# First MLP's weights read once and kept as 32-bit floats; Fourier folds by rows of 96

## The chip, the cores and the metric

The kernel runs on one core of one Trainium2 chip. The metric is the device time of one launch in microseconds (us), the median of three runs. The engines are named as the profile names them: PE (TensorE, matmuls), DVE (VectorE), ACT (ScalarE), POOL (GpSimd) and SP (SyncE, which only issues transfers). Each engine works its own instructions strictly in order; an instruction that waits holds up all that stand behind it on that engine.

## What is computed

Four batches of 768 tokens, 8 heads of 48, so 384 channels. A delta rule along the sequence gives the attention's output; then come two blocks with an MLP of 384 to 1536 to 384 channels each. The first mixes tokens by a product of rank 32 ahead of its MLP, the second by the real part of a two-dimensional Fourier transform, and normalises.

```python
for t in range(S):                                  # attention, delta rule
    kt, vt, bt = k_n[:, :, t], v[:, :, t], beta[:, :, t, None]
    y[:, :, t] = einsum('bhd,bhde->bhe', q[:, :, t], state)
    v_old = einsum('bhde,bhd->bhe', state, kt)
    state = state + bt[:, :, :, None] * einsum('bhd,bhe->bhde', kt, vt - v_old)
...
u = x + (x.transpose(0, 2, 1) @ U @ V).transpose(0, 2, 1)      # first block
x = u + np.maximum(u @ w_ch1, 0.0) @ w_ch2
...
u = x + np.real(fft(fft(x, axis=1), axis=2))                   # second block
un = (u - mean(u)) / sqrt(var(u) + 1e-06)
out = u + np.maximum(un @ w_ch1, 0.0) @ w_ch2
```

The weights U, V, `w_ch1` and `w_ch2` are stored as 64-bit floats.

## The kernel before

**Order.** Streams (Python generators, one for each kind of work) yield the modelled cost of their next instruction, and a planner (`Weave`) picks at every step which stream goes on, by modelled engine times, a bias for each stream and prices. The result is a fixed row of instructions for each engine. Rings and tiles set further waits when the program runs.

**Attention.** It has 24 chunks of 128 tokens (4 batches of 6). For each, K and Q are loaded (`s_load`, L692), normalised and folded by POOL and ACT (`s_front`), turned by transposing transfers into `BT` and `KT` (`s_turn`, L741 and L743, issued by SP) and copied (`K`, L752). Products of keys follow on PE (`ps_g`, L791 and L792), triangular blocks are spread by masks on DVE (L839: `bd`, `nf`, `t`) and the chunk is solved (`s_solve`). Its last step writes `U`; the text counts the solves by that step.

**First MLP's weights.** The two matrices have 24 pieces of 128 x 384 64-bit floats, 384 KB each; with three pieces of U and V, loads 0 to 2, that makes 3 + 24 + 24 = 51 loads. `weight_streams` has one stream that fetches into a ring `wst` of three slots (L447, issued by SP, each when the slot of the third load before is free) and one that converts. The 24 pieces go through the ring twice. In the first pass DVE looks for the largest absolute value (`peak`, L382); `weight_peak` makes a power of two for each matrix out of these. In the second pass `from_f64` makes a 32-bit float out of the two words of each value by three operations on DVE (L291, L294, L297), into `wf` or, up to late in the attention, into a PSUM scratch tile `wfp`; then the ring slot is free. `split` makes the pair of 16-bit floats that the MLP multiplies with: the high half `wh` on ACT (L364), the remainder `wl` on DVE (L367), or on ACT and POOL (L369, L370).

**First MLP.** It works on 8 blocks of 384 tokens beside the attention. For each of 12 steps PE makes `ps_h` (L1146), ACT its positive part `hh` (L1152), DVE the remainder `hl` (L1159), and PE adds the products into `acc` (L1176). The ring `wst` shares the buffer of the second block's input, so that block waits for the weights' last conversions (`s_mix`, L1245).

**Second MLP's weights.** `weight2_streams` reads its 24 pieces once: converted into tiles that stay, squared and summed on ACT (L491, the sum is read by an instruction of its own), scaled by one norm for each matrix (`weight_scale`), split in a row.

**Fourier folds.** For each batch, `fold` forms sums and differences of rows that mirror each other, in two halves i = 0 and 1 of up to 97 rows. It loads forward rows by SP and mirrored rows by POOL's gathers (L1408, one row for each partition by a table of row numbers), adds and subtracts on POOL (`pm`, L248), and ACT (L1398) and DVE (L1400) make the pair `fs`, which PE multiplies with tables (L1432). The last part of the second block (`u`, L1562; output transfers, L1569) and `s_in` (gathers `x1f`, L1408) use POOL's queue too.

Of the kernel before, what the change touches and what calls it, by code (L numbers as in the profile page):

```python
# [9 lines left out]
F32 = mybir.dt.float32  # L10
# [30 lines left out]
NP = 27  # L41
# [18 lines left out]
CU, CW1 = 7, 2  # L60
# [150 lines left out]
class Builder:  # L211
# [39 lines left out]
    def setup(self):  # L251
# [28 lines left out]
        self.wpk, self.wpk2, self.wsc1, self.unscale1 = some(2, KF), some(2), some(2), some(1)  # L280
# [4 lines left out]
    def from_f64(self, raw, f, n=HALF, sb=False):  # L285
# [11 lines left out]
        nc.vector.scalar_tensor_tensor(out=f, in0=hi, scalar=0xC0000000, in1=f,  # L297
                                       op0=ALU.bitwise_and, op1=ALU.bitwise_or)
        return f.bitcast(F32)
# [73 lines left out]
    def weight_parts(self, w1, w2):  # L373

        src = [(q, nm, j, k, x) for j in range(4) for q, (nm, xs) in enumerate(self.weight_sources(w1, w2, j)) for k, x in enumerate(xs)]

        def part(x, conv):
            return [(lambda raw: raw, self.words(x), 1092)], conv
# [6 lines left out]
        def conv(raw, done, q, nm, j, k):  # L385
            if k == 0:
                self.pair(self.wts, f"{nm}h{j}", 0, nm, j)
            sb = self.late = self.late or ("sol", NC - 2) in self.wv.mark
            f = yield from self.from_f64(raw, self.f64_tile(), sb=sb)
            done()  # L390
# [4 lines left out]
        peaks = [part(x, lambda raw, done, q=q, j=j, k=k: peak(raw, done, q, 3 * j + k)) for q, _, j, k, x in src]  # L395
        return peaks, [part(x, lambda raw, done, q=q, nm=nm, j=j, k=k: conv(raw, done, q, nm, j, k)) for q, nm, j, k, x in src]

    def weight_peak(self):

        nc = self.nc  # L400
        pk, s = self.wpk2, self.wss1
        yield {"v": 90}
        nc.vector.tensor_reduce(out=pk, in_=self.wpk, op=ALU.max, axis=AX.X)
        t = yield from self.take()
        ps = self.psu.tile([128, 130], F32, tag="psu", name="ps_w")
        yield {"p": 112}
        nc.tensor.transpose(ps[0:2, 0:128], pk, self.id32)
        top = self.wtot1
        yield {"v": 200}
        nc.vector.tensor_reduce(out=top[0:2, 0:1], in_=ps[0:2, 0:128], op=ALU.max, axis=AX.X)  # L410
        hi, p = (top[0:2, i:i + 1] for i in range(2))
        yield {"v": 70}
        nc.vector.tensor_scalar(out=p.bitcast(U32), in0=hi.bitcast(U32), scalar1=3, scalar2=0x3FFFFFFF, op0=ALU.logical_shift_left, op1=ALU.bitwise_and)
        yield {"v": 70}
        nc.vector.scalar_tensor_tensor(out=p.bitcast(U32), in0=hi.bitcast(U32), scalar=0x40000000, in1=p.bitcast(U32), op0=ALU.bitwise_and, op1=ALU.bitwise_or)
        yield {"v": 70}
        nc.vector.tensor_scalar(out=p, in0=p, scalar1=2.0 ** -60, scalar2=None, op0=ALU.max)
        yield {"v": 70}
        nc.vector.tensor_scalar(out=p.bitcast(U32), in0=p.bitcast(U32), scalar1=0x7F800000, scalar2=None, op0=ALU.bitwise_and)
        yield {"v": 70}  # L420
# [15 lines left out]
    def weight_streams(self, parts, bias):  # L436
# [1249 lines left out]
```

## Time and profile before

| | |
|---|---|
| median of 3 runs | 1136.72 us (1131.61 to 1137.6) |
| profiled run, time | 1134.32 us |
| profiled run, span of the trace | 1132.2 us |
| mean granted TensorE clock | 0.94 |
| busy in the span | PE 83%, DVE 66%, ACT 48%, POOL 30% |

The durations in this document are those of the one profiled execution. Its time is 2.1 us more than its span, and 2.4 us under the median of the runs. In the rows, an arrow in brackets ([9.81 <-DMA K<-KT]) gives the engine's idle time just before an instruction and what ended it; where an instruction waits for several things, it is the one that came last.

### The profile page before, as it was taken

The page shows a single profiled execution, that of the slowest core. Times are in us where ns is not written, and L with a number is a line of the kernel's source. Part 1 is how long each engine was busy: PE and PEld are TensorE (multiplying, and loading weights), DVE is VectorE, ACT ScalarE, POOL GpSimd, SP SyncE. Part 2 cuts the span into 40 slices and gives each one's busy share as a digit, 9 for nine tenths or more (in the row PEclk, how much of TensorE's full clock was granted, in tenths as well). Part 3 has the DMA queues.
Part 4 walks back from the last instruction along what each step waited for, and adds up shares of the span by engine and source line. Part 5 has one row for each costly group of instructions (what it writes and reads, how often), then busy time and mean ns, then how long its engine had stood idle before and what let it go on. Part 6 is the DMA issues. An engine that isn't in the chain of part 4 may idle for free. (4 is left out here: it accounts for less than half of the span.)

```text
span 1132.2 us, 25277 instructions
## 1 busy us (share of the span) xinstructions
PE 940.7 (83%) x10128; PEld 629.2 (56%) x10128; DVE 750.3 (66%) x1746; ACT 547.7 (48%) x1335; POOL 336.6 (30%) x319
## 2 busy tenths in 40 slices
PE   0377777359999888998999596899988899999998
PEld 0145655237766566766777254456656466565664
DVE  6478877889899888899984367874324453544432
ACT  4378888447665666666462133467412121222221
POOL 3322222014343233443300460365362531102010
PEclk9998787569999999999999888999999899999999
DMA  9999796837547576376322445532101411211210
GB/s 232 267 235 166 162 195 116 199 70 144 119 97 125 113 159 128 76 157 119 63 55 55 139 136 137 145 86 36 46 25 36 72 41 39 60 36 51 62 35 22
DMA packets 232974, 120.48 MB, mean 106 GB/s; under 512 B 198540, under 2 KB 218328, under 8 KB 232856
## 3 DMA queue, kind: packets, MB, share of 16 engines
q1 hardware_dynamic: 226440, 111.56, 45.9%
q0 software_dynamic: 6416, 7.30, 2.3%
q8 instruction: 79, 1.29, 0.5%
q14 instruction: 39, 0.32, 0.1%
HBM read 63.89 MB, written 14.16 MB: 69 GB/s over the span
## 5 line engine op out<-in xcount | busy, mean ns | idle before, releaser
L1176 PE MATMUL acc<-w2s,hh 128*128 128x384 f16 x1152 | 285.7, 330 | 7.8 <-DVE u L1562 5.2
L1146 PEld LDWEIGHTS <-w1s 128*128 128x128 f16 x1728 | 164.5, 99 | 137.4 <-issue 42.8
L1159 DVE SCALAR_TENSOR_TENSOR hl<-ps_h,hh 128x384 f16<-128x384 f32 x192 | 106.2, 553 | 176.0 <-ACT hh L1152 175.7
L1152 ACT ACTIVATE hh<-ps_h 128x384 f16<-128x384 f32 x192 | 93.5, 488 | 240.8 <-PE ps_h L1146 237.4
L1146 PE MATMUL ps_h<-u,w1s 128*128 128x384 f16 x864 | 176.1, 336 | 32.3 <-DVE hl L1159 23.3
L1176 PE MATMUL acc<-w2s,hl 128*128 128x384 f16 x576 | 189.6, 329 | 3.6 <-DVE hl L1159 3.6
L1146 PE MATMUL ps_h<-uh,w1s 128*128 128x384 f16 x864 | 159.7, 329 | 0.0
L1176 PEld LDWEIGHTS <-hh 128*128 128x128 f16 x1152 | 107.5, 100 | 70.0 <-issue 6.1
L248 POOL TENSOR_TENSOR GPl<-g,GPh 128x512 f16<-128x512 f32 x63 | 76.1, 1208 | 174.2 <-ACT GPh L241 161.7
L859 PEld LDWEIGHTS <-bd 128*128 128x128 f16 x1728 | 72.0, 99 | 49.2 <-DVE bd L839 21.8
L1176 PEld LDWEIGHTS <-hl 128*128 128x128 f16 x576 | 56.8, 99 | 43.2 <-DVE hl L1159 4.8
L792 PE MATMUL ps_g<-K,BT 128*128 128x256 f16 x192 | 55.1, 307 | 15.5 <-DMA K<-KT 15.5
L791 PE MATMUL ps_g<-KT,BT 128*128 128x256 f16 x192 | 54.8, 304 | 10.3 <-DMA KT<-kq 7.0
L248 POOL TENSOR_TENSOR pair<-x1f,pair 128x384 f16<-128x384 f32 x24 | 22.5, 938 | 130.2 <-ACT pair L1532 130.2
L248 POOL TENSOR_TENSOR pm<-xq 97x768 f32<-97x768 f32 (+1 forms) x16 | 28.9, 1821 | 88.3 <-DMA xq<-x1d 59.3
L798 DVE TENSOR_TENSOR g<-ps_g,mask 128x512 f32<-128x512 f32 x64 | 43.7, 683 | 6.7 <-PE ps_g L792 5.5
L248 POOL TENSOR_TENSOR kq<-kq,kq 128x384 f16<-128x384 f32 x45 | 44.7, 1010 | 10.2 <-ACT kq L241 4.8
L248 POOL TENSOR_TENSOR kb<-kq,rb 128x384 f32<-128x384 f32 x20 | 17.0, 849 | 91.2 <-DVE rb L653 57.5
L859 PE MATMUL lanes<-R,bd 128*128 128x32 f16 x768 | 34.8, 179 | 6.5 <-ACT R L241 3.7
L839 DVE TENSOR_TENSOR bd<-Xc,mmask 128x1024 f16<-128x1024 f16 x48 | 36.9, 768 | 4.5 <-ACT Xc L893 4.2
L241 ACT ACTIVATE GPh<-g 128x512 f16<-128x512 f32 x61 | 37.9, 623 | 3.7 <-DVE g L798 3.3
L248 POOL TENSOR_TENSOR kb<-kb,kb 128x384 f16<-128x384 f32 x21 | 19.9, 949 | 66.2 <-ACT kb L241 65.2
(268 smaller groups left out, 1921.5 us busy)
## 6 DMA issues: line engine op xcount, KB each, us to landing
wst<-in_moe_w_ch_dram SPq DMA_DIRECT2D x72, 384.0 KB, 3.6
K<-KT SPq DMA_DIRECT2D x48, 256.0 KB, 4.5
kq<-in_k_dram SPq DMA_DIRECT2D x24, 192.0 KB, 3.9
kq<-in_q_dram SPq DMA_DIRECT2D x24, 192.0 KB, 4.2
vt<-in_v_dram SPq DMA_DIRECT2D x24, 192.0 KB, 3.9
xnd<-vt SPq DMA_DIRECT2D x24, 192.0 KB, 2.1
xn<-xnd SPq DMA_DIRECT2D x24, 192.0 KB, 2.9
x1d<-u SPq DMA_DIRECT2D x24, 192.0 KB, 1.9
```

The costliest lines, as they stand in the source:

```text
L241: self.nc.scalar.activation(out=out, in_=in_, func=ACTF.Copy)
L248: (self.nc.vector if eng == "v" else self.nc.gpsimd).tensor_tensor(out=out, in0=in0, in1=in1, op=op)
L791: nc.tensor.matmul(o, BT[:, h, :], KT[:, :, h, :], start=i == 0, stop=False, skip_group_check=True)
L792: nc.tensor.matmul(o, BT[:, h, :], K2[:, :, h, :], start=False, stop=True, skip_group_check=True)
L798: nc.vector.tensor_tensor(out=g32.rearrange("p i (a t) -> p (i a) t", a=2), in0=ps.rearrange("p i (a t) -> p (i a) t", a=2), in1=self.mask ...
L839: self.nc.vector.tensor_tensor(out=dst.rearrange("p h (j c) -> p h j c", j=n), in0=x, in1=mask[:, None, :, :].to_broadcast(shape), op=ALU. ...
L859: nc.tensor.matmul(ps[:, h, :], lhs[:, h, :], rhs[:, h, :], start=plus is None, stop=plus is None or h == H - 1)
L1146: nc.tensor.matmul(ps[:, i, :], w[:, k, fs], u[x][:, k, :], start=(m == 0), stop=(m == 3 * KD - 1))
L1152: nc.scalar.activation(out=hh, in_=ps, func=ACTF.Relu)
L1159: nc.vector.scalar_tensor_tensor(out=hl, in0=ps, scalar=0.0, in1=hh, op0=ALU.max, op1=ALU.subtract)
L1176: nc.tensor.matmul(acc, h[:, ds_], w, start=(f == 0 and j == 0), stop=(f == KF - 1 and j == 2))
```

## The change

**Weights.** Each piece is read once. `keep` converts it; the first two of the three operations go into the scratch tile as before, the third writes a stored tile `w{p}` of 32-bit floats for the pair p. ACT squares the float into the ring slot and sums it, and then the slot is free. After the 24th piece `weight_scale` makes one norm for each matrix, and `pairs` splits the 21 stored pieces in a row; the pair p is written in the tile of stored pair p - 1. The last pair (three pieces of `w2`) is read first, for its norm alone, and once more at the end (`again`), where its split follows at once. There are 30 loads instead of 51, and the second block waits for the last of them. `CU` and `CW1` are exponents of the scales, changed for the norm.

**Folds.** Both halves load and gather 96 rows (before, the first half had loads of 97 and 96 rows and gathers of 97, the second loads of 1, 95 and 95 rows and gathers of 96). Row 192 (S/4) goes to partition 96 of the first half, by a transfer of one partition that brings both of its forward values; the other two stay zero. The transfers and gathers of a fold remain five and four. The table of row numbers follows, and the planner is told 500 and 100 ns for the loads where it was told 820.

```diff
-CU, CW1 = 7, 2
+CU = 5
...
+        out = f if out is None else out
+        nc.vector.scalar_tensor_tensor(out=out, in0=hi, scalar=0xC0000000, in1=f,
...
-        def peak(raw, done, q, i):
-            yield {"v": _v(HALF)}
-            self.nc.vector.tensor_reduce(out=self.wpk[:, q, i:i + 1], in_=raw[:, :, 1].bitcast(F32), op=ALU.max, axis=AX.X, apply_absolute_value=True)
+        def keep(raw, done, p, k):
+            j, q = divmod(p, 2)
+            if p < last and k == 0:
+                stored[p] = self.wts.tile([128, 3, HALF], U32, tag=f"w{p}", name="wf3")
+            t = tile_of()
+            f = yield from self.from_f64(raw, t, sb=self.late, out=stored[p][:, k, :] if p < last else None)
+            yield {"a": _a(HALF) + 200}
+            nc.scalar.activation(out=raw.rearrange("p n t -> p (n t)")[:, 0:HALF].bitcast(F32), in_=f, func=ACTF.Square,
+                                 accum_out=self.wpk[:, q, 3 * j + k:3 * j + k + 1])
             done()
...
+                self.pair(self.wts, f"w{(p - 1) % len(src)}", 0, nm, j)
             yield from self.split(0, nm, j, k, f, self.wsc1[:, q:q + 1], sb)
...
+        def again(raw, done, p, k):
+            t = tile_of()
+            f = yield from self.from_f64(raw, t, sb=self.late)
+            done()
+            yield from split(p, k, f, self.late)
+
+        def pairs():
+            yield from self.weight_scale(None, self.wpk, self.wsc1, self.unscale1, CW, CW, (self.wtot1, self.wss1))
+            self.wv.post("wscale1")
+            for p in range(last):
+                for k in range(3):
+                    yield from split(p, k, stored[p][:, k, :].bitcast(F32), True)
...
+        return [part(x, keep, p, k) for p in [last, *range(last)] for k, x in enumerate(src[p][1])], [part(x, again, last, k) for k, x in enumerate(src[last][1])]
...
-                    yield from self.weight_peak()
+                    yield from self.pairs()
...
-                yield ("conv", 2 * NP - 4)
+                yield ("conv", self.loads - 1)
...
+                nc.gpsimd.memset(x[96:97], 0.0)
...
-        rows = [[(0, 97, 0, 0), (1, 97, 3, HALF + 1)], [(0, 1, 0, S // 4), (1, 96, 0, 97), (1, 96, 3, HALF + 97)]]
...
-            for lo, hi, y, at in rows[i]:
-                yield _d(820)
-                nc.sync.dma_start(x[lo:hi, y, :], x1[at:at + hi - lo])
+            for y in (0, 3):
+                at = 96 * i + HALF * (y // 3)
+                yield _d(500)
+                nc.sync.dma_start(x[0:96, y, :], x1[at:at + 96])
+            if i == 0:
+                yield _d(100)
+                nc.sync.dma_start(x[96:97, 0:3:2, :], x1[S // 4:3 * S // 4 + 1:HALF])
             for y in range(2):
-                yield from self.gather(b, x[0:k, 1 + y, :], KD * B + 2 * i + y)
+                yield from self.gather(b, x[0:96, 1 + y, :], KD * B + 2 * i + y)
```

**What it moves.** The lines of the changed kernel are numbered 8 to 12 lower from `weight_streams` on (L447 is L435, L839 is L827, L1408 is L1400). First, SP's row at the start, from the first transposing transfer to the first copy of K. Before:

```order
L741 DMA_TRANSPOSE BT<-kb_131 128x8x128
L447 DMA wst<-in_moe_w_ch_dram 128x768 x2
L743 DMA_TRANSPOSE KT<-kq_127 128x16x128
L447 DMA wst<-in_moe_w_ch_dram 128x768
L692 DMA kq<-in_k_dram 128x8x48
L692 DMA kq<-in_q_dram 128x8x48
L447 DMA wst<-in_moe_w_ch_dram 128x768 x2
L752 DMA K_308<-KT 64x2048 x2
```

After:

```order
L729 DMA_TRANSPOSE BT<-kb_131 128x8x128
L731 DMA_TRANSPOSE KT<-kq_127 128x16x128
L435 DMA wst<-in_moe_w_ch_dram 128x768
L680 DMA kq<-in_k_dram 128x8x48
L680 DMA kq<-in_q_dram 128x8x48
L740 DMA K_299<-KT 64x2048 x2
```

Before, three more weight loads stand before the first transposing transfer and five between it and the first copy of K, eight in all; after, three and one.

Second, DVE's row between the sixth and the seventh solve, where L367 (after: L368) is the second half of a split, L291 to L297 are a conversion and L839 (after: L827) spreads the attention's blocks by a mask. Before:

```order
L367 SCALAR_TENSOR_TENSOR w1s<-wf,few,w1s 128x384
L291 TENSOR_SCALAR wf<-wst 128x384
L294 SCALAR_TENSOR_TENSOR wf<-wst,wf 128x384
L297 SCALAR_TENSOR_TENSOR wf<-wst,wf 128x384
L839 TENSOR_TENSOR nf_144<-Nc,mmask 128x1024
L367 SCALAR_TENSOR_TENSOR w1s<-wf,few,w1s 128x384
L291 TENSOR_SCALAR wf<-wst 128x384
L294 SCALAR_TENSOR_TENSOR wf<-wst,wf 128x384
L297 SCALAR_TENSOR_TENSOR wf<-wst,wf 128x384
L839 TENSOR_TENSOR t_151<-Tc,mmask 128x512
L367 SCALAR_TENSOR_TENSOR w2s<-wf,few,w2s 128x384
```

After:

```order
L368 SCALAR_TENSOR_TENSOR w1s<-wf_1706,few,w1s 128x384
L827 TENSOR_TENSOR nf_144<-Nc,mmask 128x1024
L368 SCALAR_TENSOR_TENSOR w1s<-wf_1706,few,w1s 128x384
L827 TENSOR_TENSOR t_151<-Tc,mmask 128x512
L368 SCALAR_TENSOR_TENSOR w2s<-wf_2586,few,w2s 128x384
L243 COPY t_151<-Zs 32x8x32
L931 STREAM_TRANSPOSE nf_144<-Zs 32x8x32
L368 SCALAR_TENSOR_TENSOR w2s<-wf_2586,few,w2s 128x384
L931 STREAM_TRANSPOSE nf_144<-Zs 32x8x32
L368 SCALAR_TENSOR_TENSOR w2s<-wf_2586,few,w2s 128x384
L1148 SCALAR_TENSOR_TENSOR hl<-ps_h,hh 128x384
```

Before, splits and conversions alternate here; after, the conversions stand further ahead and only splits are left. Counted from the start to the sixth solve, DVE has before 24 searches for the largest value, 9 conversions and 8 splits of these weights, after 24 conversions and no split (10 of the 24 ahead of the first solve, where before stand the 24 searches alone). From there to the third `hl` it has before 15 conversions and 14 splits, after 3 and 23.

Third, POOL's row in the fold of the third batch, where `xq` are the gathers, the three rows of `pm` the sums, `out_dram` output transfers. Before:

```order
L1408 DMA xq_11544<-x1d_85,rows 97x384 x2
L248 TENSOR_TENSOR pm<-xq_11544 97x2x384 x2
L248 TENSOR_TENSOR pm<-pm 97x2x191 x2
L248 TENSOR_TENSOR pm<-pm 97x2x193 x2
L1408 DMA xq_11545<-x1d_85,rows 96x384 x2
L248 TENSOR_TENSOR pm<-xq_11545 96x2x384 x2
L248 TENSOR_TENSOR pm<-pm 96x2x191 x2
L248 TENSOR_TENSOR pm<-pm 96x2x193
L1569 DMA out_dram<-u_12282,rows 3072x384
L1569 DMA out_dram<-u_12434,rows 3072x384
L1569 DMA out_dram<-u_12587,rows 3072x384
```

After:

```order
L1400 DMA xq_11493<-x1d_85,rows 96x384 x2
L248 TENSOR_TENSOR pm<-xq_11493 97x2x384 x2
L248 TENSOR_TENSOR pm<-pm 97x2x191 x2
L248 TENSOR_TENSOR pm<-pm 97x2x193 x2
L1400 DMA xq_11494<-x1d_85,rows 96x384 x2
L248 TENSOR_TENSOR pm<-xq_11494 96x2x384 x2
L248 TENSOR_TENSOR pm<-pm 96x2x191 x2
L248 TENSOR_TENSOR pm<-pm 96x2x193 x2
L1561 DMA out_dram<-u_12287,rows 3072x384
L1561 DMA out_dram<-u_12440,rows 3072x384
L1561 DMA out_dram<-u_12560,rows 3072x384
```

The gathers have 96 rows each, and the last sum of the second half, which stood behind three output transfers and a gather of `x1f`, stands ahead of them.

## Rows read from the trace of the kernel before

**Rows 1.** Page: busy sums; the span in 40 slices of 28.3 us.

```profile
PE 940.7 (83%) x10128; PEld 629.2 (56%) x10128; DVE 750.3 (66%) x1746; ACT 547.7 (48%) x1335; POOL 336.6 (30%) x319
...
PE   0377777359999888998999596899988899999998
...
GB/s 232 267 235 166 162 195 116 199 70 144 119 97 125 113 159 128 76 157 119 63 55 55 139 136 137 145 86 36 46 25 36 72 41 39 60 36 51 62 35 22
```

**Rows 2.** Busy time by stage: start and end, length, engines, clock, DMA share, GB/s.

```profile
core 0: us, PE busy (x) PEld busy (x) DVE busy (x) ACT busy (x) POOL busy (x), PEclk, DMA share, GB/s
0.00:86.30 86.30, 32.05 (x311) 18.40 (x312) 54.12 (x135) 45.85 (x108) 27.99 (x38) 1.00 1.03 244
86.30:193.70 107.40, 82.23 (x1429) 63.86 (x1427) 86.60 (x212) 91.58 (x237) 25.72 (x30) 0.81 0.88 164
193.70:255.30 61.60, 29.28 (x312) 19.36 (x312) 52.61 (x110) 31.48 (x71) 8.21 (x8) 0.59 0.57 129
255.30:620.00 364.70, 338.88 (x5278) 243.82 (x5276) 314.40 (x717) 221.42 (x547) 116.55 (x107) 1.00 0.56 109
620.00:740.00 120.00, 87.34 (x510) 53.33 (x509) 76.72 (x157) 41.02 (x117) 40.84 (x30) 0.89 0.48 134
740.00:1132.00 392.00, 370.86 (x2297) 230.44 (x2295) 165.86 (x421) 116.36 (x258) 117.32 (x108) 0.98 0.19 46
```

**Rows 3.** Timeline at the start, SP's queue and PE: start, length, instruction, idle before.

```profile
29.14 2.17 SPq L447 DMA_DIRECT2D wst<-in_moe_w_ch_dram  x2
...
39.61 0.40 PE L792 MATMUL ps_g<-K,BT 128*128 128x256 f16 x1 [9.81 <-DMA K<-KT]
```

**Rows 4.** Costs by line (sum, ns each); last two: DVE reading `wst`, by stretch.

```profile
L382 DVE TENSOR_REDUCE few<-wst 128x1 f32<-128x384 f32 x24 | 12.8, 545 | 16.9 <-DMA wst<-in_moe_w_ch_dram 16.9
...
L367 DVE SCALAR_TENSOR_TENSOR w2s<-wf,few,w2s 128x384 f16<-128x384 f32 x8 | 5.2, 654 | 1.3 <-ACT w2s L364 1.2
...
L364 ACT ACTIVATE w1s<-wfp,few 128x384 f16<-128x384 f32 x5 | 2.9, 576 | 0.0
...
L491 ACT ACTIVATE wst<-wf 128x384 f32<-128x384 f32 x24 | 12.5, 520 | 21.6 <-DVE wf L297 21.6
...
L491 ACT ACTIVATION_READ_ACCUMULATOR wst<-wf 128x1 f32 x24 | 4.5, 189 | 0.0
...
86.30:193.70 107.40, 14.72 (x27) 0.00 (x0) 0.81 0.88 164
193.70:242.30 48.60, 22.21 (x45) 0.00 (x0) 0.54 0.61 149
```

**Rows 5.** Timeline of the first fold, POOL, ACT and PE.

```profile
628.26 2.47 POOL L1408 DMA_INDIRECT xq<-x1d,rows  x1 [0.30 <-issue]
642.84 3.70 POOL L248 TENSOR_TENSOR pm<-xq 97x768 f32<-97x768 f32 x2 [12.11 <-DMA wst<-in_moe_w_ch_dram]
646.49 4.61 POOL L248 TENSOR_TENSOR pm<-pm 97x382 f32<-97x382 f32 x4
...
652.48 1.44 POOL L1408 DMA_INDIRECT xq<-x1d,rows  x1 [0.30 <-issue]
...
651.13 0.94 ACT L1398 ACTIVATE fs<-pm,few 97x772 f16<-97x772 f32 x1 [13.99 <-POOL pm L248]
...
653.74 3.04 PE L1146 MATMUL ps_h<-u,w1s 128*128 128x384 f16 x9 [13.09 <-DVE hl L1159]
```

**Rows 6.** Transfers issued, us to landing: gathers of 97 rows (877 to 883), then 96 (898 to 902).

```profile
xq<-x1d,rows POOLq DMA_INDIRECT x2, 10.5
...
xq<-x1d,rows POOLq DMA_INDIRECT x2, 3.1
```

**Rows 7.** Timeline of PE beside the folds of the third and fourth batch.

```profile
829.52 0.50 PE L1176 MATMUL acc<-w2s,hh 128*128 128x384 f16 x2 [2.37 <-ACT hh L1152]
...
854.43 0.50 PE L1432 MATMUL ps_d<-ce,fs 96*128 96x193 f16 x2 [3.70 <-ACT fs L1398]
...
901.89 0.80 PE L1176 MATMUL acc<-w2s,hh 128*128 128x384 f16 x2 [5.16 <-DVE u L1562]
```

More of the change, by code (lines that the diff above doesn't have):

```diff
@@ L373, in weight_parts, with part, tile_of, split @@
     def weight_parts(self, w1, w2):
-        src = [(q, nm, j, k, x) for j in range(4) for q, (nm, xs) in enumerate(self.weight_sources(w1, w2, j)) for k, x in enumerate(xs)]
-        def part(x, conv):
-            return [(lambda raw: raw, self.words(x), 1092)], conv
-        def peak(raw, done, q, i):
-            yield {"v": _v(HALF)}
-            self.nc.vector.tensor_reduce(out=self.wpk[:, q, i:i + 1], in_=raw[:, :, 1].bitcast(F32), op=ALU.max, axis=AX.X, apply_absolute_value=True)
+        nc = self.nc
+        src = [p for j in range(4) for p in self.weight_sources(w1, w2, j)]
+        last = len(src) - 1
+        stored = {}
+        def part(x, conv, p, k):
+            return [(lambda raw: raw, self.words(x), 1092)], lambda raw, done: conv(raw, done, p, k)
+        def tile_of():
+            self.late = self.late or ("sol", NC - 2) in self.wv.mark
+            return self.f64_tile()
+        def keep(raw, done, p, k):
[7 more added lines that the diff above has]
+                                 accum_out=self.wpk[:, q, 3 * j + k:3 * j + k + 1])
             done()
-        def conv(raw, done, q, nm, j, k):
+        def split(p, k, f, sb):
+            j, q = divmod(p, 2)
+            nm = src[p][0]
             if k == 0:
[L387 to L390, printed above, removed]
+                self.pair(self.wts, f"w{(p - 1) % len(src)}", 0, nm, j)
             yield from self.split(0, nm, j, k, f, self.wsc1[:, q:q + 1], sb)
@@ L393, in conv @@
                 self.wv.post("weights", 0, nm, j)
[L395 to L420, printed above, removed]
-        nc.vector.tensor_scalar(out=s[0:2], in0=self.id32[0:2, 0:2], scalar1=p, scalar2=None, op0=ALU.mult)
-        yield {"p": 112}
-        nc.tensor.matmul(ps[:, 128:130], self.ones[0:2], s[0:2], start=True, stop=True)
-        yield {"a": 95}
-        nc.scalar.activation(out=s, in_=ps[:, 128:130], func=ACTF.Copy)
-        self.give(t)
-        yield {"v": 70}
-        nc.vector.tensor_scalar(out=self.unscale1, in0=s[:, 0:1], scalar1=s[:, 1:2], scalar2=2.0 ** -(CW1 + CW), op0=ALU.mult, op1=ALU.mult)
-        yield {"v": 70}
-        nc.vector.reciprocal(out=self.wsc1, in_=s)
-        for q, c in enumerate((CW1, CW)):
-            yield {"v": 70}
-            nc.vector.tensor_scalar(out=self.wsc1[:, q:q + 1], in0=self.wsc1[:, q:q + 1], scalar1=2.0 ** c, scalar2=None, op0=ALU.mult)
-        self.wv.post("wscale1")
@@ L502, in weight2_streams, with weight_scale @@
         return [Stream(x(), bias) for x in (fetch, convert)]
-    def weight_scale(self, pool, squares, scale, unscale, c1, c2):
+    def weight_scale(self, pool, squares, scale, unscale, c1, c2, few=None):
         nc = self.nc
-        tot, s = (pool.tile([128, 2], F32, name=x) for x in ("wtot", "wss"))
+        tot, s = few or (pool.tile([128, 2], F32, name=x) for x in ("wtot", "wss"))
         yield {"v": 75}
@@ L1115, in attention @@
         parts = self.mix_parts() + peaks + weights
+        self.loads = len(parts)
         self.wst = self.weight_streams(parts, (WB, WB))
```

17 lines of the change are left out of this document (8 added, 9 removed).

## The prediction

> **What bounds the kernel now.** I read the page first: TensorE (PE) is busy 83% of the span, and the slices show where the other 17% lies: in the first eleven slices and again around slices 22 to 26 [rows 1]. The table of stages makes that exact [rows 2]: from 255 to 620 us PE is busy 338.9 of 364.7 us and from 740 us on 370.9 of 392, so little is to be had there except at single holes. Up to 255 us it is busy only 143.6 us, and from 620 to 740 87.3 of 120. In the first stage the transfers are the limit (DMA share 1.03, 244 GB/s). In the second VectorE (DVE) is busy 86.6 and ScalarE (ACT) 91.6 of 107.4 us: the attention's small operations and the weights share them. In the third DVE is busy 52.6 of 61.6 us and PE 29.3, at a granted clock of 0.59. So the weights matter in the first 255 us, and the Fourier folds in the holes after 620 us. The changed kernel's order tells which operations move, the trace what they cost.
>
> **Part A, the start (0 to 86 us).** The ring takes three loads at a time, and SP issues in order. Before, eight weight loads stand ahead of the first K copy; after, four (order of SP). The last two of them are issued from 29.14 us on, right ahead of K, and PE waits 9.81 us for K [rows 3]. Four loads of 393,216 bytes at the 267 GB/s of the second slice [rows 1] are 5.9 us. Against this, the 24 searches for the largest value (545 ns each, 12.8 us of DVE) go, and ten conversions with ten squares come ahead of the same point: 10 x 1.64 = 16.4 us of DVE (a conversion is three operations, 14.72 us / 9) and 10 x (0.520 + 0.189) = 7.1 of ACT [rows 4]. That is +3.6 us on a DVE that is busy 54 of 86 us, and the searches also waited 16.9 us for their loads [rows 4], so I let the slack take it. Bounds 0 (the transposes' own time sets the start) and -8 (most of the 9.81 us); I take **-5**, near the bytes.
>
> **Part B, 86 to 194 us** (up to the sixth of the 24 chunks' solves). Before, 9 conversions and 8 splits of weights stand here; after, 14 conversions with squares and no split. DVE: 14 x 1.64 less (14.7 + 8 x 0.65 for the second half of a split), that is 23.0 - 19.9 = +3.1 us. ACT: 14 x 0.709 less 8 x 0.58 (the first half), 9.9 - 4.6 = +5.3 us [rows 4]. Five more loads move 2.0 MB where the DMA share is 0.88 [rows 2]. ACT is the fuller engine, 85% busy, and I put its whole excess on the path: **+5**; bounds 0 (slack takes it) and +12 (both engines' excess, and 0.7 us of wait for each of the five loads, the 16.9 / 24 of the searches).
>
> **Part C, 194 to 255 us** (to the third `hl`, the first output block of the MLP). Before, 15 conversions (22.2 us) and 14 splits on DVE (14 x 0.65 = 9.1), 31.3 us in all; after, 3 conversions (3 x 1.48 = 4.4, from the 22.2 us of 45 operations) and 23 splits (15.0), 19.4 us [rows 4]. DVE is the busiest engine of this stage, and PE waits on the attention's chains behind it, so the 11.9 us go nearly whole. ACT gets 9 more first halves, 5.2 us, and stays below DVE: 31.5 + 5.2 of 61.6 [rows 2]. The new wait is that the 21 stored pieces can't be split until the norm is known, and that each pair is written over the stored piece ahead of it: the ACT half of a pair stands behind the DVE half of the pair before. Behind a split that waits so, DVE's order has the attention's masks and transposes, and the next chunk waits for these; 7 borders of about 1.2 us (0.58 + 0.65) would give back 8 us. Bounds -16 (the chain of the stage also tightens) and -4; I take **-11**. The last pair is read a second time at the end, 3 loads of 393 KB, counted in the 3 conversions. From there to 620 us both kernels' rows run alike and PE is full: nothing.
>
> **Part E, the first fold (625 to 654 us).** GpSimd (POOL) issues a gather of 97 rows in 2.47 us at 628.26 and then waits 12.11 us until its first sum at 642.84. The two sums take 8.3 us, ACT's `fs` starts at 651.13 having waited 13.99 us, and the MLP's `hh`, which is queued behind that `fs` on ACT, comes late, so PE stands 13.09 us [rows 5]. The view names `wst` as POOL's last releaser, but the load alone is not the gather. Gathers of 97 rows land 10.5 us after issue, those of 96 rows 3.1 [rows 6], and the small gather is issued in 1.44 us [rows 5]. With both gathers at 96 rows the landing comes 7.4 us sooner and the two issues 2 us sooner, so **-9** of the 13.09. Bounds -12 (all but about 1 us of the hole) and -3 (the two loads of 384 KB and the tables queued at the same time hold the gather up, whatever its rows).
>
> The Trainium skill, page DMA: Bandwidth & Descriptors, section "Why a DMA increments its semaphore by 16 and not by 1", says that a transfer is spread over the largest number of engines up to 16 that divides its outer dimension: 96 partitions on 16 engines, a prime such as 97 on one. The landings above agree with that. The same section names an exception, by which some of GpSimd's direct copies use 16 engines whatever the count; by it the gathers would gain nothing, and parts E to G would be about 0.
>
> **Parts F and G, the later folds.** The folds of batches 2 and 3 stand beside the second MLP, and PE waits there 2.37 us at 829.52 and 5.16 at 901.89 (`fs` of the first half late, `hh` behind it) [rows 7]. A landing 7.4 us sooner covers both: **-7.5** (bounds -7.5 and 0). In the second half PE waits 3.70 us at 854.43 for `fs` [rows 7]. Before, the last sum on POOL stands behind three output transfers and an `x1f` gather; after, in front of them (order of POOL): **-4**. Bounds -4 and +4, since those output transfers go out later, and `u` buffers come free later by about the same.
>
> The zero rows, the extra row of 96 and the shorter planner costs don't cost anything that I can find: five transfers and four gathers per fold stay, the one-row transfer replaces one of the same kind, and the memset of a single partition stands at the start of the folds.
>
> **Sum.** -5 + 5 - 11 - 9 - 7.5 - 4 = -31.5 us. Against the profiled run, 1134.3 us (1132.2 of span and 2.1 around it), that is 1102.8. The median of the three runs lies 2.4 us higher, at 1136.7: **1105** on that scale. All lower ends together give -47.5 (1089), all upper ends +9 (1146); both are unlikely together, and the range is set below.
>
> **Rivals.** About 0.5% (5.7 us) is what a measurement can tell from no change: faster is below 1131.0, slower above 1142.4.
> - *The first fold's hole stays* because the loads and tables queued with it, not the 97 rows, set its landing. For: POOL's wait is put down to `wst` [rows 5]. Against: the same gather takes 10.5 us in a stretch with hardly another transfer [rows 6]. Without E: 1105 + 9 = 1114. Chance 0.12.
> - *The weights bring nothing*: what C gives back is lost in A and B, with DVE and ACT as busy there as [rows 2] shows. For: ACT's 85%. Against: the count of operations to 255 us falls on DVE by 5 us (+3.6 + 3.1 - 11.9). The folds' -20.5 remains: 1116. Chance 0.12.
> - *The folds bring nothing*: the holes come from the sums' 8.3 us, which stay, or a gather's landing doesn't depend on its count of rows and the 10.5 us were the other transfers'. For: the sums are the longest single step of [rows 5]. Against: 10.5 and 3.1 us in [rows 6]. The weights' -11 remains: 1126. (This is what the exception in the Trainium skill's page DMA: Bandwidth & Descriptors, above, would give.) Chance 0.10, a third of it above 1131.
> - *Neither does anything* that can be measured, because the attention's own chains set the first 255 us and the MLP waits again behind each fold: 1137. Chance 0.05.
> - *More than thought*: PE's clock rises with fewer gaps from 194 to 255 us (0.59 now), and the chains tighten; with the lower bounds of A to C, 13 us more, 1085 to 1095. Chance 0.08.
> - *Slower*: the ring of three is freed only when ACT has squared a piece, and ACT stands in order behind attention work. So loads come late, and the conversions, which stand in DVE's order ahead of attention rows, hold these up. In 86 to 194 us there are 14 such loads. Each held up by 2.2 us takes the whole 31.5 us (14 x 2.2 = 31); from 2.6 us on the kernel is slower by more than 0.5%; at 3 us it is 1105 + 42 = 1147. For: DMA share 0.88 and ACT 85% busy there. Against: the searches, which waited for every load in the fullest stage, waited 0.7 us each [rows 4]. Chance 0.08.
>
> **Chances.** Forecast 0.45. Faster: 0.45 + 0.12 + 0.12 + 0.07 + 0.08 = 0.84; within 0.5%: 0.05 + 0.03 = 0.08; slower 0.08. The range 1090 to 1130 leaves out the slower case, the case without effect and half of the one with more, 0.17, and holds all others.
>
> **What would show it right or wrong.** A: PE's first K wait about 4 us, not 9.8. B and C: the sixth solve's end no later than 194, the third `hl` near 244 instead of 255, DVE's weight operations between them 19 us, ACT's idle time before squares small. E: POOL's wait before its first sum about 4 us, not 12, and PE's hole at 640 to 654 about 4. F and G: no PE wait over 1 us put down to `fs` or `hh` in the second MLP; landings of all gathers near 3 us. Wrong it would be if PE's waits in 86 to 194 us grow with `wst` as releaser in DVE's rows, if the first fold's hole stays with gathers that land in 10 us, or if the holes return elsewhere in the MLPs with PE's busy sum the same and the span unchanged.

## The result, and the profile after

The changed kernel takes 1102.0 us (median of 4 runs, 1100.6 to 1108.3), the kernel before 1135.9 beside it: ratio 0.9718, 95% interval 0.9671 to 0.9765. That is 34 us less; 1105 was predicted, with 1090 to 1130 around it. A second measurement of the same kernel (below, after_again) gave 0.9686, 0.9651 to 0.9720. The profiled run has a span of 1100.7 us, 31.5 less than before.

The page of the changed kernel, the lines of [rows 1]:

```profile
PE 945.0 (86%) x10127; PEld 633.1 (58%) x10127; DVE 747.5 (68%) x1735; ACT 555.1 (50%) x1372; POOL 330.0 (30%) x320
...
PE   0477776679999989998999889789999999999998
...
GB/s 229 221 172 151 203 159 139 122 41 150 115 102 110 86 181 118 86 147 121 71 38 66 131 154 142 150 94 29 56 11 67 78 29 37 65 29 58 58 37 22
```

For stages that can be compared, I cut both traces at the same points of the program: the first solve, the sixth, the MLP's third `hl`, the last solve, the first MLP's step 96, the end. Of before (columns as in [rows 2]):

```profile
0.00:86.27 86.27, 32.02 (x311) 18.40 (x312) 54.09 (x134) 45.82 (x108) 27.96 (x37) 1.00 1.03 244
86.27:193.71 107.44, 82.26 (x1430) 63.86 (x1427) 86.64 (x213) 91.62 (x237) 25.75 (x30) 0.81 0.88 164
193.71:255.27 61.56, 29.25 (x312) 19.32 (x312) 52.58 (x110) 31.44 (x71) 8.21 (x8) 0.59 0.57 129
255.27:615.10 359.83, 334.01 (x5214) 240.51 (x5212) 313.03 (x715) 220.03 (x545) 116.55 (x107) 1.00 0.56 110
615.10:796.39 181.29, 147.89 (x916) 91.83 (x915) 109.92 (x242) 80.84 (x206) 73.19 (x62) 0.92 0.41 111
796.39:1132.20 335.81, 315.21 (x1955) 195.28 (x1952) 134.07 (x338) 77.97 (x173) 84.97 (x77) 0.98 0.17 43
```

And of the changed kernel:

```profile
0.00:77.94 77.94, 32.00 (x299) 18.62 (x299) 55.80 (x140) 51.05 (x129) 28.60 (x38) 1.00 0.99 211
77.94:187.05 109.11, 81.01 (x1447) 62.68 (x1448) 91.65 (x213) 94.79 (x253) 28.57 (x30) 0.80 0.78 167
187.05:245.92 58.87, 37.95 (x455) 26.17 (x454) 46.88 (x107) 39.63 (x94) 7.83 (x7) 0.67 0.36 79
245.92:604.46 358.54, 328.05 (x5035) 234.77 (x5032) 309.35 (x699) 210.22 (x519) 118.98 (x108) 0.98 0.53 107
604.46:781.81 177.35, 155.56 (x940) 96.00 (x939) 109.57 (x242) 81.54 (x208) 68.12 (x62) 0.92 0.41 115
781.81:1100.70 318.89, 310.48 (x1964) 194.87 (x1961) 134.28 (x339) 77.82 (x172) 77.90 (x76) 1.00 0.17 44
```

The second column is the stage's length: -8.3, +1.7, -2.7, -1.3, -3.9 and -16.9 us. The cuts aren't points of equal work, though: PE's counts show that the changed kernel is ahead in the attention at the third `hl` (455 instructions in the stage instead of 312) and one MLP step behind at the last solve. So PE's idle time, length less busy time, is the better account: 54.3 to 45.9 us (-8.3), 25.2 to 28.1 (+2.9), 32.3 to 20.9 (-11.4), 25.8 to 30.5 (+4.7), 33.4 to 21.8 (-11.6), 20.6 to 8.4 (-12.2). That is -35.9 in all, and PE's busy time is 4.4 us higher.

### The profile page after: what moved, and what is told of

The parts are those of the page before. It is cut to its first block, busy times and chain, and to the rows that moved or that the text cites. A ratio compares the mean times of both kernels' runs of the same rounds, so it can differ in the third digit from the quotient of the medians.

```text
span 1100.7 us, 25252 instructions
## 1 busy us (share of the span) xinstructions
PE 945.0 (86%) x10127; PEld 633.1 (58%) x10127; DVE 747.5 (68%) x1735; ACT 555.1 (50%) x1372; POOL 330.0 (30%) x320
## 5 line engine op out<-in xcount | busy, mean ns | idle before, releaser
L248 POOL TENSOR_TENSOR GPl<-g,GPh 128x512 f16<-128x512 f32 x63 | 79.6, 1264 | 172.2 <-ACT GPh L241 167.3
L248 POOL TENSOR_TENSOR pm<-xq 97x768 f32<-97x768 f32 (+1 forms) x16 | 28.8, 1816 | 65.2 <-DVE u L1296 45.9
L780 PEld LDWEIGHTS <-BT 128*128 128x128 f16 x192 | 20.5, 107 | 36.8 <-DMA K<-KT 19.1
L827 DVE TENSOR_TENSOR bd<-Xc,mmask 128x1024 f16<-128x1024 f16 x48 | 36.8, 769 | 6.9 <-ACT Xc L881 6.5
L248 POOL TENSOR_TENSOR kq<-kq,kq 128x384 f16<-128x384 f32 x43 | 40.5, 962 | 3.3 <-ACT GPh L241 1.7
```

The lines of the kernel that those rows point to most:

```text
L248: (self.nc.vector if eng == "v" else self.nc.gpsimd).tensor_tensor(out=out, in0=in0, in1=in1, op=op)
L780: nc.tensor.matmul(o, BT[:, h, :], K2[:, :, h, :], start=False, stop=True, skip_group_check=True)
L827: self.nc.vector.tensor_tensor(out=dst.rearrange("p h (j c) -> p h j c", j=n), in0=x, in1=mask[:, None, :, :].to_broadcast(shape), op=ALU. ...
```

## Experiments: the two halves of the change

**folds_only** is the kernel before with the three functions of the folds changed as in the diff (the blocks from `fft_pools`, `fold` and `_constants`), and nothing else. 

> The kernel before with the change to the Fourier folds alone; the weights are read twice as before. Theory 1 (each part's gain lies where its holes closed: 11.6 us of PE's idle time less from the end of attention to the end of the first MLP, 12.2 less behind it, and 4.7 us of matmul time from the clock): 24 to 28 us off, 1108 to 1112, ratio about 0.977. Theory 2 (the division of the prediction: E, F and G 20.5 us): about 1115, ratio 0.982. Rival (the holes closed because the weights' change moved the work beside them): within 8 us of before.

It takes 1107.1 us, before 1134.3: ratio 0.9765, 0.9711 to 0.9820, 27 us less. **weights_only** is the changed kernel with these three functions as before. 

> The changed kernel with the Fourier folds as before (97 rows); the weights are read once. Theory 1 (the 19.9 us gained by the seventh solve are mostly given back until the end of attention, where 10.7 are left and one MLP step more is still to do): 4 to 9 us off, 1127 to 1132, ratio about 0.994. Theory 2 (A, B and C as predicted): 11 us off, 1125, ratio 0.990. Rival (the trace's early gain is all kept): 17 to 20 us off, 1117.

It takes 1128.9 us, ratio 0.9946, 0.9928 to 0.9963: 5 to 6 us less. The two ratios multiplied give 0.9712; the whole change has 0.9718. So the halves add up, without help from each other, and four fifths of the gain are the folds'. The prediction had 20.5 for the folds and 11 for the weights, theory 1 had both about right.

## Experiments: which transfers of 97 rows were slow

The prediction laid E to G on the gathers. Three kernels put 97 rows on one queue only, with the same order on every engine.

**gather97** 

> The changed kernel, the same order on every engine, but the gathers of each fold's first half take 97 rows again (the last one a row of zeros); the direct loads keep 96. Theory 1 (the gathers' landing sets the folds' time): landings of about 10 us again, the hole of the first fold back to 11 to 14 us, and 15 to 28 us of the change lost, 1117 to 1130, ratio to before 0.985 to 0.995. Rival (the direct loads of 97 rows were the slow ones): under 5 us lost, 1102 to 1107.

```diff
-                yield from self.gather(b, x[0:96, 1 + y, :], KD * B + 2 * i + y)
+                yield from self.gather(b, x[0:k, 1 + y, :], KD * B + 2 * i + y)
...
+    rows[96, KD * B:KD * B + 2] = S
```

1124.6 us, ratio 0.9914: 22 us of the gain gone. But part of it was the edit's own: its second gather writes the row that the one-row load writes, and waits for it (49 us on POOL in the second fold), and one value of row 96 is a zero in it. **gather97b** mends that. 

> As gather97, but without the wait that gather97 had added by itself (there the second gather of 97 rows wrote over a row that the one-row load also writes, and stood 49 us on GpSimd for it in the second fold). Now the row comes from the gather, and the one-row load brings only the other value. Theory 1 (the landing of 97 gathered rows sets the folds, 10 us instead of 3): 10 to 20 us over the changed kernel, 1112 to 1122, ratio to before 0.979 to 0.988. Rival (most of gather97's loss was its own added wait): under 8 us, up to 1110.

```diff
-                nc.sync.dma_start(x[96:97, 0:3:2, :], x1[S // 4:3 * S // 4 + 1:HALF])
+                nc.sync.dma_start(x[96:97, 0, :], x1[S // 4:S // 4 + 1])
...
+    rows[96, KD * B] = S
```

1120.3 us, ratio 0.9866, 0.9826 to 0.9906: still 18 us over the changed kernel, so theory 1 holds and the added wait was the smaller part. The issues and landings of gather97b in its last fold (865 to 872 us), and of the changed kernel in its last fold's second half (863 to 867), where two gathers of 96 rows stand:

```profile
xq<-x1d,rows POOLq DMA_INDIRECT x2, 10.9
```

```profile
xq<-x1d,rows POOLq DMA_INDIRECT x2, 2.7
```

PE's hole in the first fold of gather97b:

```profile
642.39 3.04 PE L1135 MATMUL ps_h<-u,w1s 128*128 128x384 f16 x9 [10.85 <-DVE hl L1148]
```

**loads97** leaves the gathers at 96 rows. 

> The changed kernel, the same order, but the direct loads of each fold's first half take 97 rows and the one-row load is left out (so row 96 of that half isn't the right one); the gathers keep 96. Theory 1 (the gathers set the landing): under 6 us lost, 1102 to 1108, since the direct loads are issued ahead of the gathers. Rival (direct loads of 97 rows land as late as gathers of 97 did): 10 to 28 us lost, 1112 to 1130.

```diff
-                nc.sync.dma_start(x[0:96, y, :], x1[at:at + 96])
+                nc.sync.dma_start(x[0:k, y, :], x1[at:at + k])
...
-                nc.sync.dma_start(x[96:97, 0:3:2, :], x1[S // 4:3 * S // 4 + 1:HALF])
```

1113.9 us, ratio 0.9828, 0.9790 to 0.9866: 12 us of the gain gone, so theory 1 fell here and the rival is right: direct loads of 97 rows are slow too. But loads97 does not bring back the loads of the kernel before. It has two loads of 97 rows (145.5 KB each) in the first half of a fold; the kernel before had one of 97 and one of 96 rows (145.5 and 144.0 KB). In the second half it has two loads of 96 rows, the kernel before had two of 95. So its 12 us are not the price of the direct loads before, and its first fold, below, shows an upper end. The timelines of loads97, of SP and POOL in the first two folds and of PE behind the first:

```profile
697.93 1.03 SPq L1365 DMA_DIRECT2D xq<-x1d  x2
...
627.00 1.80 POOL L248 TENSOR_TENSOR pm<-xq 97x768 f32<-97x768 f32 x1 [10.95 <-DMA xq<-x1d]
...
713.76 1.80 POOL L248 TENSOR_TENSOR pm<-xq 97x768 f32<-97x768 f32 x1 [58.37 <-DMA xq<-x1d]
...
637.11 0.48 PE L1135 MATMUL ps_h<-u,w1s 128*128 128x384 f16 x1 [9.36 <-DVE hl L1148]
```

The same load and sum of the second fold in the kernel before, and in the changed kernel:

```profile
710.75 0.28 SPq L1376 DMA_DIRECT2D xq<-x1d  x1
...
720.92 1.81 POOL L248 TENSOR_TENSOR pm<-xq 97x768 f32<-97x768 f32 x1 [45.40 <-DMA xq<-x1d]
```

```profile
694.55 0.89 SPq L1365 DMA_DIRECT2D xq<-x1d  x2
...
699.00 1.81 POOL L248 TENSOR_TENSOR pm<-xq 97x768 f32<-97x768 f32 x1 [45.92 <-DVE u L1296]
```

In this fold the gathers are issued some 40 us earlier, so the sum waits for the direct loads alone. From their issue to the sum it takes 15.8 us with two loads of 97 rows, 10.2 with one, and 4.5 with none (where the sum waits for DVE by then). While the sum of loads97 waits, the columns of [rows 2] read:

```profile
701.50:706.00 4.50, 4.42 (x29) 2.66 (x28) 3.29 (x12) 2.33 (x9) 0.00 (x0) 1.00 0.07 25
```

The core's 16 DMA engines are busy 7% in this stretch, about as much as one of 16 would be, and move 25 GB/s; at that rate the two loads take 11.9 us, an estimate from this row and their size. The rule that the prediction quoted (the Trainium skill, DMA: Bandwidth & Descriptors, "Why a DMA increments its semaphore by 16 and not by 1": an outer dimension of 96 goes to 16 engines, a prime such as 97 to one) fits both queues here; its exception, stated for some direct copies of GpSimd, did not show in these gathers.

In the first fold PE's hole is 9.36 us with two slow loads alone, 10.85 with two slow gathers alone (gather97b), 13.09 with two slow gathers and one slow load [rows 5], and 3.95 with neither. Mending the loads alone would have taken 2.2 of the 9.1 us. What mending the gathers alone would have taken no run shows; by loads97 it is at least 3.7, since that has one slow load more than the kernel before.

## Experiments: what bounds the first 250 us

Five kernels add one cost each to the changed kernel; in all but loads_twice every other row of the order stays. They ask which engine or queue sets the time of each stage, and whether a time lost there is still lost at the end.

**search_back** 

> The changed kernel with the 24 searches for the largest value put back on DVE, each just ahead of the conversion of its piece, their results unused; the order is otherwise the same on every engine. 24 x 0.545 = 13 us more on DVE before the sixth solve. Theory 1 (DVE and ACT bound 78 to 187 us, and what is lost there is partly taken up before the end of attention): the sixth solve 5 to 10 us later, the end 2 to 7 us, 1104 to 1109. Rival (slack takes it): under 2 us. Rival (all is on the path): 13 us, 1115.

```diff
+            nc.vector.tensor_reduce(out=self.wpk2[:, 0:1], in_=raw[:, :, 1].bitcast(F32), op=ALU.max, axis=AX.X, apply_absolute_value=True)
             t = tile_of()
```

1100.9 us, ratio 0.9717: no loss. The search is there (DVE's groups by line of search_back):

```profile
L393 DVE TENSOR_REDUCE few<-wst 128x1 f32<-128x384 f32 x24 | 13.0, 543 | 0.0
```

13.0 us more on DVE, and the sixth solve comes at 186.5 us (changed kernel 187.05). Slack takes it: these 13 us of DVE bound nothing up to there. The 12.8 us that the change took off DVE by dropping the search were worth nothing in themselves.

**loads_twice** 

> The changed kernel with each of the 24 pieces of weights read a second time into the ring, nothing computed from the second read but a maximum of four words that frees the slot; planned anew, so the order differs somewhat. Six weight loads stand ahead of the first copy of K instead of four. Theory 1 (reading once is worth what the start gains, 2 to 8 us): first solve 3 to 6 us later, the end 2 to 8 us, 1104 to 1110. Rival (the second reads were hidden): under 2 us. Rival (the ring is the bound up to 187 us): over 10 us.

```diff
+        def idle(raw, done, p, k):
+            yield {"v": 60}
+            nc.vector.tensor_reduce(out=self.wpk2[:, 0:1], in_=raw[:, 0:4, 1].bitcast(F32), op=ALU.max, axis=AX.X)
+            done()
...
+        return [y for p in [last, *range(last)] for k, x in enumerate(src[p][1]) for y in (part(x, keep, p, k), part(x, idle, p, k))], [part(x, again, last, k) for k, x in enumerate(src[last][1])]
```

1118.1 us, ratio 0.9862: 16 us lost, more than theory 1 gave it. Its first solve comes at 83.3 us (+5.4), the sixth at 187.3 (+0.2), but with another order between them, so it doesn't tell reads from the new plan. **reads_again** does. 

> The changed kernel, the same order on every engine, with 24 more transfers on SP: right behind the load of each piece of weights, the same 384 KB go from the weights to a spare place in DRAM, and nobody waits for them. It costs what loads_twice cost without a new plan, a conversion or a search. Theory 1 (transfers are the bound up to the sixth solve, which is why 13 us more of DVE work cost nothing there): first solve 3 to 6 us later, sixth solve 6 to 14, the end 6 to 16, 1108 to 1118. Rival (loads_twice lost its 16 us by its new plan): under 4 us, up to 1106.

```diff
                     self.nc.sync.dma_start(dst(raw), src)
+                if 3 <= n < NP:
+                    self.nc.sync.dma_start(self.spare[n - 3], src)
...
+        self.spare = [self.dr.tile([128, HALF, 2], U32, name=f"spare{n}") for n in range(24)]
```

1115.8 us, ratio 0.9805, 0.9759 to 0.9850: 14.6 us over the changed kernel on the same chip (1101.2), 0.6 us for each of the 24 transfers, though nobody waits for them. The first solve comes at 86.35 us (+8.4), the sixth at 199.44 (+12.4), and nothing of that is given back. PE's rows at the start of reads_again, and below them the changed kernel's, each followed by SP's row of the first copy of K:

```profile
30.72 0.37 PE L781 MATMUL ps_g<-KT,BT 128*128 128x256 f16 x1 [8.80 <-DMA KT<-kq]
37.41 0.40 PE L782 MATMUL ps_g<-K,BT 128*128 128x256 f16 x1 [6.32 <-DMA K<-KT]
...
28.57 0.51 SPq L437 DMA_DIRECT2D spare<-in_moe_w_ch_dram  x1
...
30.74 2.39 SPq L742 DMA_DIRECT2D K<-KT  x2
```

```profile
34.10 0.39 PE L780 MATMUL ps_g<-K,BT 128*128 128x256 f16 x1 [7.77 <-DMA K<-KT]
...
26.18 2.37 SPq L740 DMA_DIRECT2D K<-KT  x2
```

So more transfers on SP cost time up to the sixth solve, where 13 us more on DVE don't. Whether it is their bytes or their place in SP's row, this run can't tell. Each copy also takes SP 0.5 us or more to issue: 8.0 us for the 13 ahead of the first solve, about what that solve loses, and 14.7 us for all 24. And what is late is the issue of K; from there to PE's first matmul on K it takes 6.7 us here and 7.9 in the changed kernel. For the bytes speaks the DMA share, 0.99 in the changed kernel's first stage; against the bytes alone, that this stage can move more than the 211 GB/s of the changed kernel:

```profile
0.00:86.35 86.35, 32.22 (x299) 18.62 (x299) 56.13 (x140) 51.36 (x129) 28.52 (x38) 1.00 1.04 245
```

These copies are also written to DRAM, so 0.6 us is an upper end for one read that the change saved.

**split_again** adds to DVE behind the sixth solve. 

> The changed kernel with the DVE half of each of the 21 first splits done twice, the same order otherwise: 21 x 0.65 = 13.7 us more on DVE between about 180 and 245 us. Theory 1 (DVE is the bound of that stage, and the time that the weights' change gained there is given back later because PE is nearly full): the third hl 10 to 14 us later, the end only 3 to 8 us, 1105 to 1110. Rival (what is gained or lost in that stage stays to the end): 10 to 14 us at the end too, 1112 to 1116. Rival (DVE isn't the bound there): the third hl under 4 us later.

```diff
             yield from self.split(0, nm, j, k, f, self.wsc1[:, q:q + 1], sb)
+            if p < last:
+                nc.vector.scalar_tensor_tensor(out=self.wt[0, nm + 'l', j][:, k, :], in0=f, scalar=self.wsc1[:, q:q + 1], in1=self.wt[0, nm + 'h', j][:, k, :], op0=ALU.mult, op1=ALU.subtract)
```

1115.1 us, ratio 0.9835, 0.9806 to 0.9864; against the changed kernel's two measurements 13 us more. The stage from the sixth solve to the third `hl` in split_again:

```profile
186.57:257.16 70.59, 36.97 (x452) 24.96 (x452) 59.31 (x129) 39.95 (x94) 7.82 (x7) 0.66 0.30 66
```

It is 11.7 us longer than in the changed kernel, DVE's busy time is 12.4 us more (59.31 against 46.88), and the last solve is 12.0 us later too (616.45 against 604.46). So DVE does bound this stage, as part C said, and the rival that what is lost here stays to the end is right; theory 1, that it would be given back, fell.

**hl_again** adds to DVE between the third `hl` and about 420 us. 

> The changed kernel, the same order, with the hl of the MLP's steps 4 to 27 made twice on DVE: 24 x 0.553 = 13.3 us more on DVE between about 250 and 420 us. Theory 1 (DVE is the bound there as well, and PE isn't; so the lead of 20 us at the seventh solve ran into DVE's row): 9 to 13 us later at the end of attention and at the end, 1111 to 1115. Rival (PE is the bound there, as the prediction had it: both kernels' rows alike and PE full): under 4 us, up to 1106.

```diff
                         nc.vector.scalar_tensor_tensor(out=hl, in0=ps, scalar=0.0, in1=hh, op0=ALU.max, op1=ALU.subtract)
+                        if wi == 0 and 3 <= s < 27:
+                            nc.vector.scalar_tensor_tensor(out=hl, in0=ps, scalar=0.0, in1=hh, op0=ALU.max, op1=ALU.subtract)
```

1110.7 us, ratio 0.9774: 9.5 us over the changed kernel (1101.2). The stretch from the third `hl` to the last solve in hl_again:

```profile
243.71:611.22 367.51, 333.46 (x5038) 236.52 (x5036) 322.84 (x722) 210.44 (x518) 118.32 (x108) 0.97 0.51 105
```

It takes 367.5 us, 9.0 more than in the changed kernel (single profiles of kernels with this order give 355.0 to 363.8). So of the 13.4 us added to DVE about two thirds come through here, and seven tenths at the end. Of the 9.0 us, 3.6 are idle time of PE, and 5.4 are longer matmuls (333.46 us against 328.05, for 5038 and 5035 of them), at a granted clock of 0.97 against 0.98. PE is busy 91% there in the changed kernel (328.05 of 358.54 us), and it is still not the bound alone: the prediction's "PE is full: nothing" is wrong for this stretch.

## An experiment for a faster version

**split_pool** 

> The changed kernel, the same order, with every third split's second half made by ACT and GpSimd instead of DVE: 8 x 0.65 = 5.2 us less on DVE between 180 and 250 us, 8 instructions more on ACT (about 0.4 to 0.6 us each, 4 us) and on GpSimd (about 1 us each), which is busy 7.8 of 59 us there. Theory 1 (DVE is the bound of that stage and the time stays to the end): the third hl 3 to 5 us sooner, the end 3 to 5 us, 1097 to 1099, faster than both kernels. Rival (ACT becomes the bound, or the longer way over two engines holds the splits up): no gain, or up to 4 us slower.

```diff
         e = yield {"w": _v(HALF), "g": _a(HALF) + 94 + _g(HALF)} if sb else {"v": _v(HALF)}, "side"
+        if i == 0 and sb and k == 1:
+            e = "g"
```

**after_again** is the changed kernel, run beside it. 

> The changed kernel itself on the same chip, for comparison with split_pool: 1100 to 1104, ratio to before 0.970 to 0.974.

split_pool takes 1103.2 us (ratio 0.9707, 0.9670 to 0.9744), after_again 1101.2 (0.9686, 0.9651 to 0.9720): no difference that can be told. The rows of the splits from 180 to 250 us, of split_pool and then of after_again:

```profile
L372 ACT ACTIVATE wf<-wf,few 128x384 f32<-128x384 f32 x9 | 5.5, 615 | 0.3
L370 DVE SCALAR_TENSOR_TENSOR w1s<-wf,few,w1s 128x384 f16<-128x384 f32 x8 | 5.2, 651 | 2.8 <-ACT w1s L365 2.6
L370 DVE SCALAR_TENSOR_TENSOR w2s<-wf,few,w2s 128x384 f16<-128x384 f32 x7 | 4.4, 627 | 3.5 <-ACT w2s L365 3.5
```

```profile
L368 DVE SCALAR_TENSOR_TENSOR w1s<-wf,few,w1s 128x384 f16<-128x384 f32 x12 | 7.4, 613 | 1.0 <-ACT w1s L365 0.9
L368 DVE SCALAR_TENSOR_TENSOR w2s<-wf,few,w2s 128x384 f16<-128x384 f32 x11 | 6.7, 612 | 2.6 <-ACT w2s L365 2.6
```

DVE's splits fall from 14.1 to 9.6 us, but DVE then waits 6.1 instead of 3.5 us for ACT's first halves, since ACT has 5 us more to do ahead of them. The third `hl` comes at 247.4 us instead of 245.2. The rival held: work can't simply be moved from DVE to ACT there.

## Why the prediction came out

**A, -5: the sign and the place right, the mechanism not settled, the measure 8.3.** The first solve comes 8.3 us sooner, in weights_only too (77.95 us), so it isn't the folds'. The first K matmul starts 5.5 us sooner (34.10 against 39.61), near the 5.9 that I took from the bytes of four loads. But PE's wait for K only fell from 9.81 to 7.77, where about 4 was foretold: KT came sooner too, so the wait moved with it. And what moved is the issue of K in SP's row, 5.2 us sooner than before:

```profile
31.36 1.17 SPq L752 DMA_DIRECT2D K<-KT  x2
```

From issue to matmul it is 8.2 us before and 7.9 after. That SP reaches K sooner is shown; whether through fewer bytes ahead of it or through fewer issues isn't (reads_again adds both).

**B, +5: the sign right, the reason half wrong.** The stage is 1.7 us longer. DVE's share of the price was nothing (search_back), and SP's transfers, which I had only as an upper bound of 0.7 us for a load, do cost time there (reads_again). That ACT's excess of 5.3 us makes up the 1.7 wasn't tested.

**C, -11: the stage right, the end wrong.** From the sixth to the seventh solve the changed kernel gains 13 us (its seventh solve is at 225.98, before 245.85, 19.9 us sooner), PE's idle time in the stage falls by 11.4 us, and split_again shows that DVE is the bound. But the third `hl` comes only 9.4 us sooner, and weights_only ends 5 to 6 us sooner where A, B and C together said 11. The step that failed is "From there to 620 us both kernels' rows run alike and PE is full: nothing". What is added to DVE there costs time as well (hl_again), and PE has 4.7 us more of idle time in it. The view of PE's waits between the third `hl` and the last solve (sum, times, longest), before and after, shows the largest part:

```profile
PE ps_g L792 <- DMA K<-KT: 2.1, 4, 0.8
```

```profile
PE ps_g L780 <- DMA K<-KT: 6.4, 7, 2.1
```

It is no accident of one run: the ten profiles with the weights read in the new way and the order unchanged there or nearly so have 4.3 to 7.6 us of this wait and 28.6 to 32.6 us of PE's idle time in the stage; before and folds_only have 2.1 and 2.7, and 25.8 and 27.0. Why the copies of K come late wasn't settled; no run changed SP's row or the transposes ahead of them alone. Nor does it make up the whole. By idle time the weights' part would still be 12 us (-8.3 + 2.9 - 11.4 + 4.7). The rest is in PE's busy time up to step 96, 625.4 us before and 634.6 after for the same matmuls, a sum that lies between 627 and 637 in the runs that share its order, so that I can't say what share of it the clock has (0.67 in the stage into which part of the attention moved; from the third `hl` to the last solve 0.98, before 1.00).

**E, -9: the size right, the cause half.** PE's hole in the first fold went from 13.09 to 3.95 us, 9.1 less. ACT and PE in the changed kernel, the rows that answer to [rows 5]:

```profile
632.65 0.94 ACT L1390 ACTIVATE fs<-pm,few 97x772 f16<-97x772 f32 x1 [5.85 <-POOL pm L248]
...
634.61 0.65 PE L1135 MATMUL ps_h<-u,w1s 128*128 128x384 f16 x3 [3.95 <-DVE hl L1148]
```

The landing of the gathers, 7.4 us sooner by [rows 6], was taken as the whole reason. But slow gathers alone make a hole of 10.85 us (gather97b) where the kernel before had 13.09, so 2.2 of the 9.1 us hang on the direct loads, and I had priced them at nothing ("five transfers and four gathers per fold stay"). The change moved both, so the sum held. POOL's wait before its first sum fell from 12.11 to 5.98 us, where about 4 was foretold. The rival that the tables and `wst` hold the landing up is no more than a remainder: the gathers of that fold land in 5.1 us, against 2.7 in a quiet stretch.

**F and G, -11.5: too small.** All three holes of [rows 7] are gone; in the changed kernel 0.4 us of PE's waits behind the first MLP's step 96 are put down to `fs` and none to `hh`. The stretch is 16.9 us shorter: 12.2 us less idle time, near the 11.5 predicted, and 4.7 us less busy time for the same matmuls. That is the term that I left out. It isn't chance: of six runs with this order behind step 96 five have 310.5 us of PE's busy time there and one 312.2, before 315.2 and weights_only 316.3, both with holes. Before, in stretches around the second and the third hole:

```profile
835.00:850.00 15.00, 15.00 (x94) 9.05 (x93) 4.60 (x9) 2.45 (x5) 6.47 (x6) 1.00 0.07 27
850.00:860.00 10.00, 5.74 (x26) 3.52 (x25) 2.98 (x6) 1.81 (x3) 3.96 (x4) 0.83 0.20 61
860.00:895.00 35.00, 35.00 (x237) 23.74 (x235) 16.37 (x45) 9.01 (x22) 12.23 (x9) 1.00 0.32 44
...
898.33:901.89 3.56, 0.00 (x1) 0.11 (x2) 2.47 (x5) 1.70 (x3) 2.36 (x2) 0.69 0.18 49
901.89:906.00 4.11, 4.11 (x14) 1.87 (x13) 1.46 (x3) 0.00 (x0) 0.00 (x0) 0.50 0.51 174
906.00:910.00 4.00, 4.00 (x24) 2.35 (x23) 0.56 (x1) 0.49 (x1) 0.71 (x1) 0.93 0.47 137
```

PE stands from 896.7 to 901.89 us, the granted clock falls to a mean of 0.69 in that time, and the first 4.11 us of work behind the hole go at 0.50, that is at 1.2 GHz: 14 matmuls in 4.11 us, where 94 take 15.00 at full clock, about 26 in the same time. So the hole costs nearly 2 us behind its end. After the change PE is busy without a break from 781.8 to 870 us, at a clock of 1.00.

**The sum** was -31.5 and the profiled spans differ by 31.5, but that is partly luck: the folds gave about 27 instead of 20.5, the weights 5 to 6 instead of 11. Of the slower rival, a ring that holds the attention up, DVE's row has no trace: DVE's groups by line up to the sixth solve show 0.2 us of wait before the first operation of 24 conversions, and none that a load ended:

```profile
L291 DVE TENSOR_SCALAR wfp<-wst 128x384 uint32<-128x384 uint32 (+2 forms) x24 | 13.0, 541 | 0.2
```

SP does wait for the ring: up to 190 us its weight loads stand 24.6 us for ACT's squares (before, 16.8 us for the searches and conversions), and all that stands behind them in SP's row waits too. What that costs no run shows. The view of SP's waits in the changed kernel:

```profile
SPq L435 <- ACT wst L395: 24.6, 16, 8.2
```

## What to carry to other kernels

A gain at a milestone isn't a gain at the end until the same work has been done on both sides: 20 us of lead at the seventh solve came down to 5 or 6, in part because the next stage hung on more than the engine that the view of PE alone suggested. Adding a known cost to one engine with the order kept (13 us of DVE: nothing ahead of the sixth solve, nearly all right behind it) showed the bound of a stage where busy shares had misled. It tells only as much as the cost is pure: the copies of reads_again took SP's time and the DMA engines' at once. And where an operation waits for two transfers of the same bad shape, both have to be priced; mending the loads alone would have brought a quarter (13.09 to 10.85 us, of 13.09 to 3.95).

## What the runs showed of the hardware

Loads of 97 rows issued by SP are slow, as gathers of 97 rows issued by GpSimd are: from issue to the sum that waits for the loads 15.8 us with two of them and 10.2 with one (4.5 with 96 rows only), and 10.9 us to landing for the gathers (2.7 with 96). While the sum waits for two such loads, the core's DMA engines are for 4.5 us busy 7% and move 25 GB/s. A gather of 97 rows also takes GpSimd 2.15 to 2.47 us to issue, one of 96 mostly 0.92. A hole of 5 us on TensorE cost nearly 2 us more behind its end, at a granted clock of 0.50 for 4 us (4.7 us of matmul time for the three holes together). And 24 copies of 384 KB from DRAM to DRAM, which nothing waits for, cost the kernel 0.6 us each, their issue on SP included (median 0.53 us), while the DMA share was 0.99 in the first 78 us.
